# A chunked RWKV-7 recurrence with a SoLU layer behind it: whole products in the first doubling, transfers moved behind the read-out, a mean from a view, loads reordered

## The chip, the cores and the metric

The kernel runs on one core of one Trainium2 chip. The metric is the device time of one execution in microseconds (us); lower is better. A profile of one execution gives, for each engine, when each instruction ran and what it waited for. The engines are TensorE (PE for its matmuls, PEld for its weight loads), VectorE (DVE), ScalarE (ACT), GpSimd (POOL) and SyncE (SP), which issues nearly all DMA transfers here. A "q" behind a name (SPq, DVEq) is the engine's sequencer.

## The reference

A recurrence over 768 time steps, for 4 batches and 8 heads with a state of 40 x 40 each, is followed by a feed-forward layer on the 3072 rows of its output.

```python
for t in range(S):                       # r, k, v, w, a, b: (4, 8, 768, 40)
    y[:, :, t] = np.einsum('bhd,bhde->bhe', rt, state)
    Sa = np.einsum('bhde,bhe->bhd', state, at)
    state = state * wt[:, :, None, :] - np.einsum('bhd,bhe->bhde', Sa, bt) \
            + np.einsum('bhd,bhe->bhde', vt, kt)
x = y.transpose(0, 2, 1, 3).reshape(3072, 320)
h = x @ w_in                             # 320 -> 1024
sm = softmax(h)
solu = h * sm
ln = (solu - mean(solu)) / sqrt(var(solu) + 1e-6) * g_ln
out = ln @ w_out                         # 1024 -> 320
```

## The kernel before

**Chunks and rounds.** Time is cut into 12 rounds of 64 steps. A round's rows are loaded once, and it is worked in two chunks, each of two batches (the two halves of the 128 partitions) and all 8 heads. So there are 24 chunks, i = 0 to 23, and chunk i belongs to round i // 2. Inside a chunk the recurrence is written as matrix products. That needs, for each head and batch, the inverse of a 64 x 64 triangular matrix whose strict part is called nt.

**The stages of a chunk.** Each is a generator, and every `yield` ends a step:
- `front(i)`, five chunks ahead: logarithm of w (L334), cumulative sums on TensorE and their exponentials (pcum, pcx, L338 to L354), b and k scaled on POOL (L341), a copied on POOL (L371), a transposed (paT, evicted by DVE at L382), b transposed, nt (L292).
- `scatter` and `gather` write a round's nt to DRAM and bring its diagonal blocks back with one block in each partition.
- `invert(n)`: elimination on DVE in small steps (`prod`, `u`). Rounds 0 to 3 (`invert_fine`) do it for 16 x 16 blocks (14 pairs of steps), then ACT copies the result to u and ut (L441), and both go to DRAM (L443). Later rounds eliminate 32 x 32 blocks.
- `bring_inverse(i)` fetches the blocks as tinv and tinvT: eight transfers for a chunk.
- `solve(i)` doubles the inverse on TensorE: for the first rounds from 16 to 32 (py16, then pz16), for all from 32 to 64 (py, then pz). In the first doubling ACT evicts py16 to y_mid (L555); DVE adds the lower left part into tinv (L561, two instructions) and ACT writes the upper right part into tinvT (L565, four instructions). Both read the bank of pz16.
- `attend(i)`: transposes of k, v, r and the products that need no state (kT, vT, psi, rT, lamv, px0).
- `recurrence(i)` and `readout(i)`: the part that needs the state sm; its product nuT gives plamu, which comes once for each chunk and serves here as its mark in time. `readout` ends in x (L678), the chunk's y times the decays. x holds one round and has one buffer.
- `repack(n)` moves a round's x to xT, twelve transfers (L689 to L692), once both chunks of it are read out.
- `hidden(m)` and `output(m)`, six chunks behind (LAG = 6): h, softmax, product, statistics; then transposes (plnT) and the products with w_out (po). `centre()` folds g_ln and the mean over the features into w_out once, at chunk 6.
- `weights()` turns w_in and w_out from 64-bit numbers into 32-bit ones piece by piece (`narrow`), from a landing buffer of four pieces, with transfers three pieces ahead (L215).

**What sets the order.** The whole body is under a manual schedule: each engine, and each DMA queue, does its instructions in the order in which the program emits them. Strings of letters say how the steps of the stages interleave in a chunk: `EARLY` for chunks 0 to 5 and `STEADY` from 6. A letter is one step: r recurrence, y read-out, a `attend(i + 1)`, s `solve(i + 1)`, f and g fronts, I inverse (a number of steps given by `inverse_steps`), W weights, L loads, h hidden, b and o the end of the hidden layer and the output. An instruction that has to wait holds everything behind it on its engine. The small products of `solve` and the transposes share two PSUM banks (`bank`), so a bank that is not evicted holds TensorE.

Of the kernel before, what the change touches and what calls it, by code (L numbers as in the profile page):

```python
# [26 lines left out]
def shape_constants():  # L27

    s, t = np.arange(L)[:, None], np.arange(L)[None, :]
    first = (s < L // 2).astype(np.float64)
    two = np.eye(2)
    parts = dict(  # L40
        ident=np.eye(P),
        tri=np.concatenate([s < t, s < t], 0),
        cum_in=np.kron(two, first - (s <= t)),
        cum_ex=np.kron(two, (s < t) - first),
        half=np.concatenate([np.kron(two, 1 - first), np.kron(two, first)], 1),
        low=-1.0 * (np.arange(P)[:, None] % Q >= Q // 2),
    )
    at, where = 0, {}
    for name, x in parts.items():
        where[name] = (at, at + x.shape[1])  # L50
        at += x.shape[1]
    return np.concatenate([np.asarray(x, np.float64) for x in parts.values()], 1).astype(np.float32), where
# [3 lines left out]
def kernel(  # L56
# [37 lines left out]
    const = ctx.enter_context(tc.tile_pool(name="const", bufs=1))  # L94
    raw = ctx.enter_context(tc.tile_pool(name="raw", bufs=1))
    two = ctx.enter_context(tc.tile_pool(name="two", bufs=2))
    small = ctx.enter_context(tc.tile_pool(name="small", bufs=4))
    dram = ctx.enter_context(tc.tile_pool(name="dram", bufs=2, space=bass.MemoryType.DRAM))
    ps1 = ctx.enter_context(tc.tile_pool(name="ps1", bufs=2, space=PSUM))
    psd = ctx.enter_context(tc.tile_pool(name="psd", bufs=2, space=PSUM))  # L100
# [22 lines left out]
    def c_(name):  # L123
        lo, hi = where[name]
        return cst[:, lo:hi]
# [17 lines left out]
    x0_t = zeroed(nc.vector, "x0", [P, H, 64], 2, True)  # L143
    ti_t = zeroed(nc.vector, "tinvT", [P, 2, G, L], 2)
    tn_t = [const.tile([P, H, 2, Q // 2], FP32, name=f"tinv{i}") for i in range(2)]
    y_mid = const.tile([P, 2, G, Q], FP32, name="y_mid")
    w_in = const.tile([P, 5, DFF // 2], FP32, name="w_in")
    w2 = const.tile([P, NF, DM], FP32, name="w2")
    g_rows = const.tile([NF, P], FP32, name="g_rows")
    g_col = const.tile([P, NF], FP32, name="g_col")  # L150

# [86 lines left out]
    def centre():  # L238

        pg = bank("pg")  # L240
        nc.tensor.transpose(out=pg[:, 0:NF], in_=g_rows, identity=ident[0:NF, 0:NF])
        nc.scalar.copy(out=g_col, in_=pg[:, 0:NF])
        gb = two.tile([P, NF, P], FP32, tag="e", name="gb", bufs=1)
        nc.scalar.mul(out=gb, in_=g_col.unsqueeze(2).to_broadcast([P, NF, P]), mul=1.0 / DFF)
        yield
        t = bank("mean")
        for c in range(NF):
            nc.tensor.matmul(t[:, 0:DM], lhsT=gb[:, c, :], rhs=w2[:, c, :], start=c == 0, stop=c == NF - 1)
        mean = two.tile([P, DM], FP32, tag="osb", name="mean", bufs=1)
        nc.scalar.copy(out=mean, in_=t[:, 0:DM])  # L250
        yield
        for c in range(NF):
            nc.vector.scalar_tensor_tensor(out=w2[:, c, :], in0=w2[:, c, :], scalar=g_col[:, c:c + 1],
                                           in1=mean, op0=ALU.mult, op1=ALU.subtract)
            if c % 2:
                yield

    def half(p):
        return slice(64 * p, 64 * p + 64)
# [59 lines left out]
    def given(i, name):  # L319
        return of_round[i // 2][name][:, i % 2]  # L320
# [36 lines left out]
    def quarter(q):  # L357
        return slice(Q * q, Q * q + Q)
# [6 lines left out]
    def front(i):  # L365

        d = st[i]
        a = d["a"] = a_t[i % 2]
        parts = decay(i)
        next(parts)  # L370
        nc.gpsimd.tensor_copy(out=keyed(a)[:, :, :, 0:D], in_=by_heads(given(i, "a")))  # L371
        yield
        for _ in range(2):
            next(parts)
            yield
        next(parts)
        yield
        ax = d["ax"]
        t = bank("paT")
        for g in range(G):  # L380
            nc.tensor.transpose(out=t[:, g * P:(g + 1) * P], in_=pair(a, g), identity=ident)
        nc.vector.tensor_tensor(out=ax[:, :, 0:P], in0=t.rearrange("p (g t) -> p g t", g=G), in1=ax[:, :, P:2 * P],  # L382
                                op=ALU.mult)
        yield
        bT = transposed("bT", d["kb"][:, 1])
        yield
        n, s = divmod(i, 2)
        if s == 0:
# [27 lines left out]
    def invert_fine(n):  # L416
# [21 lines left out]
        for key, t, src in (("ut", ut, x.rearrange("b c t -> b t c")), ("u", u, x)):  # L438
            dst = of_round[n][key] = dram.tile([64, Q, Q], FP32, tag=key + "_dram", name=key + "_dram")
            for z in range(2):  # L440
                nc.scalar.copy(out=t[half(z)][:, :, R * z:R * z + R], in_=src[half(z)])  # L441
            for z in range(2):
                nc.sync.dma_start(out=dst[:, R * z:R * z + R, :], in_=t[half(z)])  # L443
        yield
# [80 lines left out]
    def solve(i):  # L525
# [20 lines left out]
        def whole(q):  # L546

            return (lambda p, g: nt[quarter(q), p, g, quarter(q % 2)],
                    lambda p, g: tinv[quarter(q), G * p + g].rearrange("s z c -> s (z c)"),
                    lambda p, g: tinvT[quarter(q), p, g, quarter(q % 2)],  # L550
                    lambda p, g: y_mid[quarter(q), p, g, :])

        if fine:
            t = products("py16", [(q, whole(q)[0], whole(q)[1]) for q in range(4)])
            nc.scalar.copy(out=y_mid, in_=t[:, 0])  # L555
            yield
            t = products("pz16", [(q, whole(q)[3], whole(q)[2]) for q in range(4)],
                         [(q, whole(q)[2], whole(q)[3]) for q in (0, 2)])
            for q in (0, 2):
                x = tinv[quarter(q), :, 0].rearrange("s (p g) c -> s p g c", p=2)  # L560
                nc.vector.scalar_tensor_tensor(out=x, in0=t[quarter(q), 1, :, :, 0:R], scalar=c_("low")[quarter(q)],  # L561
                                               in1=x, op0=ALU.mult, op1=ALU.add)
            for q in range(4):
                rows, c = slice(Q * q, Q * q + R), Q * (q % 2) + R
                nc.scalar.mul(out=tinvT[rows, :, :, c:c + R], in_=t[rows, 0, :, :, R:Q], mul=-1.0)  # L565
            yield

        def left(q):
# [201 lines left out]
    def fronts(i):  # L770

        return [j for j in ((4, 5) if i == 0 else (i + AHEAD,)) if j < N]

    EARLY = ("r r a W I r f W r r I W y r W a s f L a W I s W a f a W s I f a W s I f W f",
             "r r a W I r f W r r I g W y r I W a s f g L W a s a f g W a s f g W s a f g W f g W")
    STEADY = "r b r a r f b b o r o I o r o y o r I o h a f L a s a h f a I h f s h f h a f h"
    front_of = {}
    idle = ps2.tile([P, DFF], FP32, tag="h", name="idle")

# [19 lines left out]
    def warm(n, x):  # L799

        for _ in range(n):
            nc.tensor.matmul(idle[:, 0:512], lhsT=x[:, 0:P], rhs=x, start=True, stop=True)

    def later(n):
        load(n, "b", "k")
        yield

    with tc.manual_schedule():
# [14 lines left out]
        load(0, "r")  # L823
        gather(0)
        load(1, "k")
        turns("a f g a a f f W a g g", {}, f=f, g=g, a=at, W=ws)
        load(2, "w", "a")
        turns("I a I f g f g I f g", dict(I=[3, 4, 4]), f=f, g=g, I=inv, a=at)
        load(1, "v", "r")
        scatter(1)  # L830
        load(2, "b", "k")
        gather(1)
        turns("I a", dict(I=99), a=at, I=inv)
        warm(3, of_round[0]["spilt"])
        bring_inverse(0)
        begin(0)
        inv = inverses()
        turns("s W W W W s I s s I", dict(I=[4, 4]), s=so, I=inv, W=ws)
        after, before = None, None
        for i in range(N):  # L840
            m, more, js = i - LAG, i + 1 < N, fronts(i)
# [1 line left out]
            parts = dict(r=recurrence(i), y=readout(i), I=inv, W=ws, h=now, b=after, o=before)  # L843
            if i == LAG:
                steps(ws, 99)
                parts["o"] = centre()
            parts.update(zip("fg", (front_of[j] for j in js)))
            if more:
                parts.update(a=attend(i + 1), s=solve(i + 1))
# [4 lines left out]
            if i % 2 == 0:  # L854
                load((i + 6) // 2, "w", "a")
                parts["L"] = later((i + 6) // 2)
            turns(EARLY[len(js) - 1] if i < LAG else STEADY, dict(I=inverse_steps(i), s=2 if i == LAG else 1), **parts)
            if i % 2:
                if i + 2 < N:
                    bring_inverse(i + 2)  # L860
                load((i + 3) // 2, "v", "r")
                repack(i // 2)
            if js and js[-1] % 2:
                scatter(js[-1] // 2)
            begin(i + 1)
            after, before = now, output(m) if m >= 0 else None
        for m in range(N - LAG, N):
            now = hidden(m)
            turns("b h h o o h h b b h h o o o o", {}, h=now, b=after, o=before)
            after, before = now, output(m)  # L870
# [31 lines left out]
```

## Time and profile before

| | before |
|---|---|
| time, median of 3 runs | 742.56 us (741.05 to 743.6) |
| span of the profiled execution | 737.8 us |
| PE busy | 633.8 us (86%) |
| DVE busy | 432.0 us (59%) |
| ACT busy | 279.3 us (38%) |
| POOL busy | 102.0 us (14%) |
| mean granted TensorE clock | 0.905 |

The page's slices are 40 equal parts of the span (18.4 us each); a digit is a busy share in tenths, and PEclk is the clock that TensorE was granted, in tenths of full speed. In a row of the timeline stand the start, the duration, the engine, the line of the code, the operation and its tiles, and in brackets how long the engine sat idle before it and what ended the idle time. Rows of SPq are the issue of transfers, not the movement of their data. plamu of chunks 0 to 7 begins at 65.1, 91.8, 121.4, 156.1, 180.0, 214.7, 241.7 and 276.6 us.

### The profile page before, as it was taken

The page shows a single profiled execution, that of the slowest core. Times are in us where ns is not written, and L with a number is a line of the kernel's source. Part 1 is how long each engine was busy: PE and PEld are TensorE (multiplying, and loading weights), DVE is VectorE, ACT ScalarE, POOL GpSimd, SP SyncE. Part 2 cuts the span into 40 slices and gives each one's busy share as a digit, 9 for nine tenths or more (in the row PEclk, how much of TensorE's full clock was granted, in tenths as well). Part 3 has the DMA queues.
Part 4 walks back from the last instruction along what each step waited for, and adds up shares of the span by engine and source line. Part 5 has one row for each costly group of instructions (what it writes and reads, how often), then busy time and mean ns, then how long its engine had stood idle before and what let it go on. Part 6 is the DMA issues. An engine that isn't in the chain of part 4 may idle for free.

```text
span 737.8 us, 27981 instructions
## 1 busy us (share of the span) xinstructions
PE 633.8 (86%) x12165; PEld 451.7 (61%) x12165; DVE 432.0 (59%) x1186; ACT 279.3 (38%) x662; POOL 102.0 (14%) x192
## 2 busy tenths in 40 slices
PE   7547878388396879999999999999999899988997
PEld 4525657267375656776676767766676566554554
DVE  3417455355245756958869678598685872333442
ACT  4224634245342243435334443435243333322222
POOL 4211020120110102211122012202110000000000
PEclk9756887687676989999999999999999999999999
DMA  9874534643544425454553655545514322000001
GB/s 157 152 127 97 105 67 79 135 80 71 109 89 85 75 44 98 78 110 87 104 97 66 109 99 93 98 92 100 99 30 89 66 54 40 20 20 23 17 3 35
DMA packets 269866, 58.95 MB, mean 80 GB/s; under 512 B 255528, under 2 KB 265392, under 8 KB 269744
## 3 DMA queue, kind: packets, MB, share of 16 engines
q1 hardware_dynamic: 266480, 56.44, 41.0%
q8 instruction: 96, 1.57, 0.9%
q10 hardware_dynamic: 3264, 0.72, 0.6%
q14 instruction: 26, 0.21, 0.1%
HBM read 39.03 MB, written 13.37 MB: 71 GB/s over the span
## 4 chain that ended last, share of the span: by engine, by line
PE 61%; DVE 12%; ACT 6%; SPq 6%; issue 4%; DMA 3%; DVEq 0%; ACTq 0%
PE po L744 13%; PE h L699 12%; PE pyo L671 4%; PE plnT L739 3%; PE pcx L351 3%; DVE prod L465 3%; PE pz L539 2%; DVE u L467 2%; PE py L539 2%; PE plamv L290 2%; DVE nmax L709 2%; PE pcum L338 2%; DMA blk<-blk_dram 2%; PE ppsi L290 2%; PE pyo L593 2%
## 5 line engine op out<-in xcount | busy, mean ns | idle before, releaser
L699 PE MATMUL h<-w_in,xT 128*128 128x512 f32 (+1 forms) x288 | 128.6, 636 | 3.9 <-DVE e L716 3.9
L744 PE MATMUL po<-w,lnT 128*128 128x320 f32 x384 | 115.6, 440 | 0.0
L744 PEld LDWEIGHTS po<-w,lnT 128*128 128x128 f32 x384 | 69.5, 192 | 26.4 <-issue 3.3
L467 DVE TENSOR_TENSOR u<-u,prod 128x30 f32<-128x30 f32 (+7 forms) x240 | 65.1, 271 | 8.2
L465 DVE TENSOR_TENSOR prod<-blk,u 128x30 f32<-128x30 f32 (+7 forms) x240 | 65.5, 273 | 7.1
L351 PE MATMUL pcx<-cst,lw 128*128 128x132 f32 x192 | 35.0, 316 | 37.5 <-ACT tinvT L565 31.1
L341 POOL TENSOR_TENSOR kx<-raw_b,inv 128x320 f32<-128x320 f32 x24 | 20.7, 867 | 289.7 <-ACT inv L339 227.4
L351 PEld LDWEIGHTS pcx<-cst,lw 128*128 128x128 f32 x192 | 29.5, 214 | 47.1 <-ACT tinvT L565 35.0
L709 DVE TENSOR_REDUCE nmax<-h 128x1 f32<-128x1024 f32 x24 | 29.3, 1221 | 47.9 <-PE h L699 47.9
L699 PEld LDWEIGHTS h<-w_in,xT 128*128 128x128 f32 (+1 forms) x288 | 38.0, 190 | 31.4 <-issue 29.4
L678 DVE TENSOR_TENSOR x<-pyo,kx 128x512 f32<-128x512 f32 x24 | 16.6, 691 | 69.3 <-PE pyo L671 46.8
L749 ACT ACTIVATE osb<-po,rs 128x320 f32<-128x320 f32 x24 | 12.6, 527 | 97.2 <-PE po L744 86.4
L740 ACT COPY lnT<-plnT 128x512 f32<-128x512 f32 x48 | 27.5, 586 | 33.6 <-PE plnT L739 33.5
L713 ACT ACTIVATE e<-h,nmax 128x1024 f32<-128x1024 f32 x24 | 26.7, 1114 | 34.4 <-DVE nmax L709 34.4
L292 DVE TENSOR_TENSOR lamv<-plamv,cst 128x512 f32<-128x512 f32 x24 | 16.6, 691 | 39.2 <-PE plamv L290 39.2
L716 DVE TENSOR_TENSOR e<-h,e 128x1024 f32<-128x1024 f32 x24 | 29.4, 1225 | 14.6 <-ACT e L713 14.0
L539 PE MATMUL py<-tinv,nt 32*32 32x32 f32 x1280 | 28.4, 204 | 9.1 <-DMA tinv<-ut_dram 7.4
L731 POOL TENSOR_TENSOR rs<-c,mhalf 128x1 f32<-128x1 f32 x24 | 13.2, 548 | 157.2 <-DVE c L730 157.2
L739 PE MATMUL plnT<-cst,e 128*128 128x128 f32 x192 | 29.5, 282 | 5.7 <-DVE e L716 5.4
L581 ACT ACTIVATE tinvT<-pz 32x256 f32<-32x256 f32 x48 | 17.9, 373 | 43.5 <-PE pz L539 43.2
L657 POOL TENSOR_TENSOR sm<-tot,fac 128x320 f32<-128x320 f32 x20 | 14.9, 745 | 126.3 <-DVE tot L656 109.0
L539 PEld LDWEIGHTS py<-tinv,nt 32*32 32x32 f32 x1280 | 23.6, 115 | 14.3 <-DMA tinv<-ut_dram 9.0
(121 smaller groups left out, 1181.1 us busy)
## 6 DMA issues: line engine op xcount, KB each, us to landing
blk<-blk_dram SPq DMA_DIRECT2D x16, 256.0 KB
raw_k<-in_k_dram SPq DMA_DIRECT2D x24, 160.0 KB
v<-in_v_dram SPq DMA_DIRECT2D x24, 160.0 KB
r<-in_r_dram SPq DMA_DIRECT2D x24, 160.0 KB
out_dram<-osb SPq DMA_DIRECT2D x24, 160.0 KB
raw_w<-in_w_dram SPq DMA_DIRECT2D x23, 160.0 KB
raw_b<-in_b_dram SPq DMA_DIRECT2D x23, 160.0 KB
raw_a<-in_a_dram SPq DMA_DIRECT2D x23, 160.0 KB
```

What stands on the lines that cost most here:

```text
L290: nc.tensor.matmul(t[half(c ^ p * cross), p, g * L:(g + 1) * L], lhsT=lhs[half(p), g, half(c)], rhs=rhs[half(p), g, half(c)], start=True, ...
L351: nc.tensor.matmul(t[:, g * 132:g * 132 + 132], lhsT=pair(lw, 2 * j + g), rhs=cst[:, lo:lo + 132], start=True, stop=True)
L465: nc.vector.tensor_tensor(out=t, in0=nb[:, j:j + 1, j + 1:Q].to_broadcast([P, rows, m]), in1=u[:, 0:rows, j:j + 1].to_broadcast([P, rows, ...
L467: nc.vector.tensor_tensor(out=u[:, 0:rows, j + 1:Q], in0=u[:, 0:rows, j + 1:Q], in1=t, op=ALU.subtract)
L539: nc.tensor.matmul(t[quarter(out), c:c + Q], lhsT=lhs(p, g), rhs=rhs(p, g), start=True, stop=True)
L671: nc.tensor.matmul(t[half(p), c, g * W:g * W + used], lhsT=kb[half(c), j, 2 * g + p, :], rhs=lam[half(c), h % 2, h // 2, 0:used], start=i ...
L699: nc.tensor.matmul(h[:, j * 512:j * 512 + 512], lhsT=of_round[i // 2]["xT"][rows, kt, i % 2 * P:i % 2 * P + P], rhs=w_in[rows, 4 if kt == ...
L709: nc.vector.tensor_reduce(out=nmax, in_=h, axis=AX.X, op=ALU.max, negate=True)
L716: nc.vector.tensor_tensor(out=q, in0=h, in1=e, op=ALU.mult)
L739: nc.tensor.transpose(out=t[:, j * P:(j + 1) * P], in_=q[:, f * P:(f + 1) * P], identity=ident)
L740: nc.scalar.copy(out=lnT[:, fs.start:fs.stop].rearrange("p f t -> p (f t)"), in_=t)
L744: nc.tensor.matmul(o[:, 0:DM], lhsT=lnT[:, f, :], rhs=w2[:, f, :], start=f == 0, stop=f == NF - 1)
```

## The change

It has five parts.
- **The first doubling.** A constant tile y_16 has the right half of a unit matrix in its right columns. One DVE instruction evicts py16 into its left columns, with the unit matrix added and the sign set (`low` is -1 for the lower rows and 0 for the upper). The products of pz16 with y_16 are then whole: both results are plain copies, on ACT, and DVE no longer adds into tinv.
- **Transfers of y.** `repack` gets a letter of its own, X, directly behind the read-out of an odd chunk, in place of its call at the chunk's end behind the transfers of the next inverse and the loads.
- **The mean of w_out.** The matmuls of `centre` take g_col as weights through a view that repeats one column 128 times, in place of a tile gb that ACT filled; the factor 1/1024 moves to the mean's eviction. The first step of `centre` comes at the end of chunk 5.
- **The start.** The first inverse is emitted in one piece, before the steps of the fronts that surrounded it; its transfers come before scatter and loads of round 1; the loads of round 2's w and a come earlier, others later; five warm-up matmuls replace three.
- **Orders.** In `EARLY` a step of `attend` (r transposed) stands ahead of pz16; in chunk 6 the four steps of `solve` are spread. The copy of a moves one step later in `front`. The pool `small` has 3 buffers in place of 4.

```diff
+        one=np.kron(np.ones((4, 1)), np.eye(Q)),
...
-    small = ctx.enter_context(tc.tile_pool(name="small", bufs=4))
+    small = ctx.enter_context(tc.tile_pool(name="small", bufs=3))
...
+    y_16 = const.tile([P, H, Q], FP32, name="y_16")
+    nc.scalar.copy(out=y_16[:, :, Q // 2:], in_=c_("one")[:, Q // 2:].unsqueeze(1).to_broadcast([P, H, Q // 2]))
...
-        gb = two.tile([P, NF, P], FP32, tag="e", name="gb", bufs=1)
-        nc.scalar.mul(out=gb, in_=g_col.unsqueeze(2).to_broadcast([P, NF, P]), mul=1.0 / DFF)
...
-            nc.tensor.matmul(t[:, 0:DM], lhsT=gb[:, c, :], rhs=w2[:, c, :], start=c == 0, stop=c == NF - 1)
+            nc.tensor.matmul(t[:, 0:DM], lhsT=g_col[:, c:c + 1].to_broadcast([P, P]), rhs=w2[:, c, :], start=c == 0, stop=c == NF - 1)
...
-        nc.scalar.copy(out=mean, in_=t[:, 0:DM])
+        nc.scalar.mul(out=mean, in_=t[:, 0:DM], mul=1.0 / DFF)
...
         next(parts)
+        yield
+        next(parts)
         nc.gpsimd.tensor_copy(out=keyed(a)[:, :, :, 0:D], in_=by_heads(given(i, "a")))
         yield
-        for _ in range(2):
-            next(parts)
-            yield
+        next(parts)
+        yield
...
-                nc.scalar.copy(out=t[half(z)][:, :, R * z:R * z + R], in_=src[half(z)])
+                if n == 0 and key == "ut":
+                    nc.vector.tensor_copy(out=t[half(z)][:, :, R * z:R * z + R], in_=src[half(z)])
+                else:
+                    nc.scalar.copy(out=t[half(z)][:, :, R * z:R * z + R], in_=src[half(z)])
...
-                    lambda p, g: y_mid[quarter(q), p, g, :])
+                    lambda p, g: y_16[quarter(q), G * p + g, :])
...
-            nc.scalar.copy(out=y_mid, in_=t[:, 0])
+            nc.vector.scalar_tensor_tensor(
+                out=y_16[:, :, 0:R], in0=t[:, 0].rearrange("q p g c -> q (p g) c")[:, :, 0:R], scalar=c_("low"),
+                in1=c_("one")[:, 0:R].unsqueeze(1).to_broadcast([P, H, R]), op0=ALU.mult, op1=ALU.add)
...
-            for q in (0, 2):
-                x = tinv[quarter(q), :, 0].rearrange("s (p g) c -> s p g c", p=2)
-                nc.vector.scalar_tensor_tensor(out=x, in0=t[quarter(q), 1, :, :, 0:R], scalar=c_("low")[quarter(q)],
-                                               in1=x, op0=ALU.mult, op1=ALU.add)
             for q in range(4):
                 rows, c = slice(Q * q, Q * q + R), Q * (q % 2) + R
-                nc.scalar.mul(out=tinvT[rows, :, :, c:c + R], in_=t[rows, 0, :, :, R:Q], mul=-1.0)
+                nc.scalar.copy(out=tinvT[rows, :, :, c:c + R], in_=t[rows, 0, :, :, R:Q])
+            for q in (0, 2):
+                nc.scalar.copy(out=tinv[quarter(q), :, 0].rearrange("s (p g) c -> s p g c", p=2),
+                               in_=t[quarter(q), 1, :, :, 0:R])
...
-    EARLY = ("r r a W I r f W r r I W y r W a s f L a W I s W a f a W s I f a W s I f W f",
-             "r r a W I r f W r r I g W y r I W a s f g L W a s a f g W a s f g W s a f g W f g W")
-    STEADY = "r b r a r f b b o r o I o r o y o r I o h a f L a s a h f a I h f s h f h a f h"
+    EARLY = ("r r a W I r f W r r I W y r X W a s f L a W I a s W f a f W s I a f W s I f W",
+             "r r a W I r f W r r I g W y r I W a s f g L W a a s f g W a f g W s a f g W s f g W")
+    STEADY = "r b r a r f b b o r o I o r o y o r X I o h a f L a s a h f a I h f s h f h a f h"
...
-        turns("a f g a a f f W a g g", {}, f=f, g=g, a=at, W=ws)
         load(2, "w", "a")
-        turns("I a I f g f g I f g", dict(I=[3, 4, 4]), f=f, g=g, I=inv, a=at)
-        load(1, "v", "r")
+        turns("a f g a a f f a g g W", {}, f=f, g=g, a=at, W=ws)
+        turns("I a f g f g f g a", dict(I=99), f=f, g=g, I=inv, a=at)
+        warm(5, of_round[0]["spilt"])
+        bring_inverse(0)
         scatter(1)
-        load(2, "b", "k")
+        load(2, "b")
+        load(1, "v")
         gather(1)
-        turns("I a", dict(I=99), a=at, I=inv)
-        warm(3, of_round[0]["spilt"])
-        bring_inverse(0)
+        load(1, "r")
+        load(2, "k")
         begin(0)
         inv = inverses()
-        turns("s W W W W s I s s I", dict(I=[4, 4]), s=so, I=inv, W=ws)
+        turns("W W s W W s W W I s I s", dict(I=[4, 4]), s=so, I=inv, W=ws)
...
-                parts["o"] = centre()
+                parts["o"] = middle
...
+            else:
+                parts["X"] = repacked(i // 2)
+            order = EARLY[len(js) - 1] if i < LAG else STEADY
+            if i == LAG:
+                order = order.replace("a s a h f a I h f s h f h", "a s a h f s a I h f s h f s h")
+            turns(order, dict(I=inverse_steps(i)), **parts)
             if i % 2:
                 if i + 2 < N:
                     bring_inverse(i + 2)
                 load((i + 3) // 2, "v", "r")
-                repack(i // 2)
...
+            if i == LAG - 1:
+                middle = centre()
+                steps(middle, 1)
```

More of the change, by code (lines that the diff above doesn't have):

```diff
@@ L802, in warm, with repacked @@
             nc.tensor.matmul(idle[:, 0:512], lhsT=x[:, 0:P], rhs=x, start=True, stop=True)
+    def repacked(n):
+        repack(n)
+        yield
     def later(n):
@@ L856 @@
                 parts["L"] = later((i + 6) // 2)
-            turns(EARLY[len(js) - 1] if i < LAG else STEADY, dict(I=inverse_steps(i), s=2 if i == LAG else 1), **parts)
+            else:
[4 more added lines that the diff above has]
+            turns(order, dict(I=inverse_steps(i)), **parts)
             if i % 2:
```

## The prediction

> **What bounds the kernel now.** I read the page's slices first, then the busy time by stretches of one chunk each (cut where plamu, one per chunk, starts), then the waits, the timeline around the longest one, and the DMA queue's own timeline.
>
> ```profile
> PE   7547878388396879999999999999999899988997
> PEclk9756887687676989999999999999999999999999
> ```
> ```profile
> 65.00:92.00 27.00, 20.09 (x574) 16.61 (x576) 15.18 (x41) 15.35 (x41) 4.60 (x7) 0.86 0.54 106
> 92.00:121.00 29.00, 21.96 (x550) 18.29 (x546) 17.59 (x57) 11.48 (x32) 4.09 (x9) 0.71 0.33 64
> 121.00:156.00 35.00, 21.29 (x596) 17.57 (x598) 12.14 (x40) 14.02 (x39) 3.66 (x6) 0.71 0.56 111
> 156.00:180.00 24.00, 19.42 (x597) 16.16 (x593) 14.95 (x55) 11.29 (x33) 4.63 (x10) 0.79 0.35 65
> 180.00:215.00 35.00, 22.14 (x617) 18.32 (x613) 12.14 (x40) 14.13 (x38) 3.66 (x6) 0.66 0.55 107
> 277.00:658.00 381.00, 368.75 (x7250) 259.95 (x7242) 265.82 (x708) 151.06 (x349) 54.22 (x96) 1.00 0.42 79
> ```
> Columns after the length: PE, PEld, DVE, ACT, POOL, clock, DMA share, GB/s. From 277 us on TensorE is 97% busy at clock 1.00 (23.8 us a chunk): nothing in the change takes work from it there, so I expect nothing from those 461 us. Before 277 us no engine is full, the clock is 0.66 to 0.86, and chunks 2 and 4 take 35 us against 24 for chunk 3, which has the same work.
>
> ```profile
> PE pcx L351 <- ACT tinvT L565: 31.1, 6, 10.2
> ```
> ```profile
> 130.74 0.69 PE L539 MATMUL pz<-y_mid,tinvT 32*32 32x32 f32 x31 [1.51 <-issue]
> 131.36 0.66 PE L271 MATMUL prT<-cst,r 128*128 128x128 f32 x4
> 142.22 1.25 PE L351 MATMUL pcx<-cst,lw 128*128 128x132 f32 x4 [10.21 <-ACT tinvT L565]
> ```
> ```profile
> 133.98 1.38 SPq L316 DMA_DIRECT2D raw_w<-in_w_dram  x2
> 135.24 0.69 DVE L678 TENSOR_TENSOR x<-pyo,kx 128x512 f32<-128x512 f32 x1 [10.89 <-DMA xT<-x]
> 138.75 0.69 DVE L561 SCALAR_TENSOR_TENSOR tinv<-pz,cst,tinv 32x128 f32<-32x128 f32 x2
> 138.88 1.27 ACT L441 COPY ut<-u 64x256 f32<-64x256 f32 x2 [10.48 <-DVE u L435]
> 141.02 1.14 ACT L565 ACTIVATE tinvT<-pz 16x128 f32<-16x128 f32 x4
> ```
> The last releaser is not the cause. TensorE waits for a bank read by L565; ACT is held in order at L441 by the inverse on DVE; DVE stands at L678, because x has one buffer and the xT transfers of the chunk before still read it. They were issued at 123.42 to 133.88, behind everything else of the DMA queue. The same at chunk 4 (10.96 us).
>
> The start is a queue too:
> ```profile
> 38.25 2.44 SPq L399 DMA_DIRECT2D blk_dram<-nt  x4
> 44.13 1.62 SPq L409 DMA_DIRECT2D blk<-blk_dram  x2
> 45.85 1.42 SPq L443 DMA_DIRECT2D ut_dram<-ut  x2
> 49.32 1.79 SPq L486 DMA_DIRECT2D tinv<-ut_dram  x4
> ```
> The first inverse is ready at 39.0, its copies at 41.1, but its write leaves at 45.85, since scatter, loads and gather of round 1 stand before it.
>
> [...] (clock 0.50 from 135 to 140) [...] 0.50 still at 145 to 150 with PE busy 4.74 of 5. [...] here ut's issue ends at 47.27 and its reader starts at 49.32. [...] the trace has L565 begin (58.57) only after L561 ends (58.49).
>
> **Part by part.**
> *Transfers of y behind the read-out.* The 12 transfers (10.5 us of issue at chunk 1) move to directly behind x, before the second half of the chunk. x of the next chunk then finds its buffer free. At chunk 2, DVE could start x at 125.0; the following rows (x 0.69, tot 0.48, weights 1.4, psi 0.68, weights 0.5, inverse 0.35: starts overlap, 3.5 us from 135.24 to 138.75) end near 129, ACT's four copies 2.1 us later, then rT's 0.58: pcx near 132 instead of 142.2. Gain 9.7. The stretch 142 to 154 at half clock (PE busy 11 us) would at full clock take some 7: 4 more, an estimate. Chunks 2 and 4: 2 x 13.5 = 27. What is queued behind them on the DMA queue: weight fetches (three pieces ahead, as many as the rest of the chunk uses) and the next inverse's transfers, needed a chunk later.
>
> *First doubling as whole products.* One DVE instruction per chunk replaces ACT's y_mid copy (0.372); the two DVE L561 (0.34 each) become two ACT copies. Not seen in the trace: the eviction of 128x128 from PSUM. [...] upper 0.48, row L656 with 320 elements. I take 0.34. It stands behind x and before psi and the inverse, and pz16 comes two steps later, so it is hidden. L565 then no longer waits for a DVE that is in the inverse, and rT goes ahead of it. The waits this ends: 1.5 at 81.7 (chunk 0), 2.9 at 106.6 with half clock to 120 (chunk 1: 5 in all), 2.5 at 166.6 (chunk 3: 3), 2.5 at chunk 5, 4.3 and 1.2 at chunk 6. ACT's extra 0.6 before the left half's products is charged in the allowance below.
>
> *Mean from a view.* ACT gb (1.06) and its wait (0.7) go, 1.7 in chunk 6; the 16 matmuls (4.6) stay, with weights read from one column; [...] I take as now. With the solve of chunk 6 spread, chunk 6 gains 8.
>
> *Start.* The whole inverse runs at once on DVE: in round 1's rows the same 28 steps take 6.5 us, so done near 33, ut copied by DVE by 33.6, its write 12.2 us earlier. Behind it wait paT's evictions (two times 0.69) and the fronts of 2 and 3, hence TensorE idles to 34 and has 5 us of work (now 32.65 to 37.6), then five warm-up matmuls (ten passes, 0.81 each by 4.84 for six): free near 46.7. py16, its eviction, then pz16 at 48 instead of 55.9. From there to plamu 9.2 us at half clock, near 8 warm. First plamu at 56 instead of 65.1: gain 9. The fill of y_16 waits on ACT for the constants; at most 0.5 us ahead of the first Ln at 6.33.
>
> *The rest.* raw_a is freed one step later, on POOL behind grown b; the load that waits for it has a chunk of slack. small with 3 buffers: each value lives one chunk. Both cost nothing.
>
> *Sum.* 9 + 1.5 + 5 + 13.5 + 3 + 13.5 + 2.5 + 8 = 56. From it I take an allowance of 8. The DMA queue issues about 42 us for a pair of early chunks (sum of its rows from 152 to 204, without waits), while these gains would leave pairs of 42 to 46 us: it becomes nearly the bound, and some waits like that at 97.7 and 98.5 (tinv, 2.0 us at chunk 1) must appear. So 48: 742.6 - 48 = 695.
>
> **Rivals.**
> *The queue takes the place of x's wait.* The moved transfers push back fetches and tinv; each even chunk then loses some 3 us at tinv, as chunk 1 does now (idle at 96.1 and 98.1, landed at 98.5), and stays at half clock. Left: 2 x 6.5 at x, 9 at the start, 4 at chunk 6: 26, so 717. For it: 42 us of issue. Against: counted from the nt that ends an even chunk, the queue does scatter (2.8), eight inverse transfers (4), gather (2.2), xT (10.5) and fetches (2 to 4), so the next eight leave at 22 to 28, while py16 of the following chunk comes at about 29 (one chunk of 21, and 8 from nt at 152.3 to py16 at 160.3).
> *The clock stays up.* The 8 are not given back and half-clock stretches (115 to 120, 170 to 178, 227 to 240) go as well: 60 or more, 682. Against: gaps of 1.5 us put down to "issue" stay.
> *Slower.* Eviction on DVE, longer warm-up and weight fetches behind 10 us of transfers stall DVE in order, and the gain of the start is lost: about 748. Against: in-order DVE has 12 to 15 us of work in 35.
>
> **How the numbers follow.** Forecast 0.62, queue 0.20, clock 0.13, slower or nothing 0.05. The range 676 to 723 holds the first three cases, with 6 us around the outer two. Faster 0.94, same 0.02, slower 0.04.
>
> **What would show it.** DVE x waiting for xT: from 21.9 us to under 3. PE waiting for L565: from 31.1 to under 8. First plamu at 54 to 58, that of chunk 7 near 229 (276.6 now). Clock over 0.8 in 120 to 230. From there to the end 461 us as now. Wrong, if plamu of chunks 2 and 3 is still over 30 us apart, or if DMA tinv or fetches head the waits.

## The result, and the profile after

| | before | after |
|---|---|---|
| time, median of 4 runs | 742.5 us (741.05 to 743.6) | 714.0 us (711.51 to 716.53) |
| ratio to before, 95% interval | | 0.962 (0.957 to 0.966) |
| span of the profiled execution | 737.8 us | 709.6 us |
| PE busy | 633.8 us | 634.4 us |
| mean granted clock | 0.905 | 0.923 |

The change is faster by 28.5 us. TensorE is busy as long as before; what went is its idle time, 104.0 us of the span before and 75.2 after. The forecast was 695, a gain of 48.

The page's slices of after (17.7 us each), engine and clock:
```profile
PE   7566877898875999999999999999999899979997
...
PEclk9676699687899599999999999999999999999999
```
Busy time by stretches from one plamu to the next (chunks 0 to 6, then the rest to chunk 23). After the length stand PE, PEld, DVE, ACT, POOL, clock, DMA share and GB/s:
```profile
58.70:91.20 32.50, 25.10 (x569) 20.66 (x568) 18.29 (x50) 15.31 (x41) 5.39 (x8) 0.70 0.59 116
91.20:114.40 23.20, 17.71 (x565) 14.57 (x569) 15.81 (x52) 11.82 (x35) 4.33 (x9) 0.93 0.40 84
114.40:140.60 26.20, 21.63 (x602) 18.12 (x598) 13.71 (x44) 14.10 (x39) 3.88 (x6) 0.74 0.78 141
140.60:161.40 20.80, 18.95 (x594) 15.85 (x586) 14.53 (x53) 11.31 (x33) 4.69 (x10) 0.84 0.41 87
161.40:185.20 23.80, 21.45 (x602) 17.99 (x592) 12.93 (x42) 13.99 (x39) 3.76 (x6) 0.71 0.77 132
185.20:214.10 28.90, 22.39 (x612) 17.38 (x606) 12.37 (x39) 9.75 (x27) 4.63 (x8) 0.94 0.48 87
214.10:249.10 35.00, 27.06 (x613) 19.22 (x607) 22.50 (x56) 10.40 (x28) 2.21 (x5) 0.76 0.31 57
249.10:622.20 373.10, 361.05 (x7138) 254.38 (x7134) 266.19 (x703) 150.05 (x346) 54.45 (x96) 1.00 0.46 81
```
Before, these chunks took 26.8, 29.6, 34.7, 23.9, 34.7, 27.0 and 35.0 us. Chunks 1 to 4 together fell from 122.9 to 94.0. Start and chunk 0 together are what they were (91.8 and 91.2): plamu of chunk 0 comes 6.4 us earlier, and chunk 0 is 5.7 longer. Chunks 5 and 6 together rose from 62.0 to 63.9. So the whole gain lies in four chunks. Of its 28.9 us there 23.9 are idle time of TensorE (38.2 us before, 14.3 after); the other 5.0 are shorter busy time, at a mean clock of 0.80 in place of 0.71.

TensorE's longest waits up to 285 us, after (us in total, times, longest):
```profile
PE pz L545 <- issue: 12.7, 5, 7.0
PE pbT L273 <- DVE kx L385: 5.4, 1, 5.4
PE pu L639 <- DVE x L620: 4.6, 2, 3.2
PE pyo L678 <- DVE lamu L294: 3.3, 1, 3.3
PE py L545 <- DMA tinv<-ut_dram: 3.1, 2, 2.0
```
The 31.1 us of pcx behind L565 are gone, and so are the 21.9 us of DVE's x behind xT. The list shows what stands in their place. Chunk 2, at the rows that answer to those of before (x at 135.24 after a wait of 10.89, pcx at 142.22 after 10.21):
```profile
119.19 0.69 DVE L685 TENSOR_TENSOR x<-pyo,kx 128x512 f32<-128x512 f32 x1 [0.51 <-PE pyo L678]
...
124.46 1.27 ACT L447 COPY ut<-u 64x256 f32<-64x256 f32 x2 [1.54 <-DVE u L438]
...
125.94 0.24 PE L545 MATMUL pz<-tinvT,y 32*32 32x32 f32 x3 [1.67 <-issue]
...
126.61 0.59 ACT L275 COPY rT<-prT 128x512 f32<-128x512 f32 x1
...
127.25 1.25 PE L353 MATMUL pcx<-cst,lw 128*128 128x132 f32 x4 [0.16 <-ACT rT L275]
```
pcx begins 12.8 us after chunk 2's plamu, where it was 20.8. Its bank is now free as soon as rT is copied, ahead of the solve's copies. But rT itself stands on ACT behind the four copies of ut and u, so that the gap of 1.67 ahead of pz16 did not set when pcx began: without it pcx would have waited longer for rT. And the four pcx matmuls take 1.25 us, as long as before: the clock was 0.50 in both (from 142.0 to 143.5 before, from 127.0 to 128.5 after).

### The profile page after: what moved, and what is told of

It reads as the page before. It is cut to its first block, busy times and chain, and to the rows that moved or that the text cites. A ratio compares the mean times of both kernels' runs of the same rounds, so it can differ in the third digit from the quotient of the medians.

```text
span 709.6 us, 27985 instructions
## 1 busy us (share of the span) xinstructions
PE 634.4 (89%) x12169; PEld 451.3 (64%) x12169; DVE 434.2 (61%) x1180; ACT 279.1 (39%) x668; POOL 103.3 (15%) x192
## 3 DMA queue, kind: packets, MB, share of 16 engines
q8 instruction: 96, 1.57, 1.0%
## 4 chain that ended last, share of the span: by engine, by line
PE 67%; DVE 13%; ACT 5%; SPq 5%; DMA 5%; issue 5%; POOL 0%; ACTq 0%; DVEq 0%; POOLq 0%
PE po L751 15%; PE h L706 14%; PE pyo L678 5%; PE plnT L746 4%; PE pcx L353 3%; PE py L545 2%; DVE prod L471 2%; PE plamv L292 2%; PE pz L545 2%; DVE u L473 2%; DVE nmax L716 2%; SPq L318 2%; PE ppsi L292 2%; PE pyo L600 2%; PE pcum L340 2%
## 5 line engine op out<-in xcount | busy, mean ns | idle before, releaser
L706 PE MATMUL h<-w_in,xT 128*128 128x512 f32 (+1 forms) x288 | 130.4, 643 | 3.9 <-DVE e L723 3.9
L343 POOL TENSOR_TENSOR kx<-raw_b,inv 128x320 f32<-128x320 f32 x24 | 21.1, 878 | 305.0 <-ACT inv L341 270.9
L685 DVE TENSOR_TENSOR x<-pyo,kx 128x512 f32<-128x512 f32 x24 | 16.6, 691 | 46.7 <-PE pyo L678 45.8
L720 ACT ACTIVATE e<-h,nmax 128x1024 f32<-128x1024 f32 x24 | 26.8, 1116 | 34.0 <-DVE nmax L716 34.0
L545 PE MATMUL py<-tinv,nt 32*32 32x32 f32 x1280 | 26.5, 200 | 5.9 <-DMA tinv<-ut_dram 3.1
L728 DVE BATCH_NORM_STATS2 bs<-e 128x6 f32<-128x512 f32 x48 | 30.9, 685 | 0.8
L746 PEld LDWEIGHTS plnT<-cst,e 128*128 128x128 f32 x192 | 22.1, 143 | 13.9 <-ACT sT L631 4.0
```

What stands on the lines that cost most here:

```text
L545: nc.tensor.matmul(t[quarter(out), c:c + Q], lhsT=lhs(p, g), rhs=rhs(p, g), start=True, stop=True)
L706: nc.tensor.matmul(h[:, j * 512:j * 512 + 512], lhsT=of_round[i // 2]["xT"][rows, kt, i % 2 * P:i % 2 * P + P], rhs=w_in[rows, 4 if kt == ...
L728: nc.vector.bn_stats(out=bs[:, j], in_=q[:, j * 512:j * 512 + 512])
L746: nc.tensor.transpose(out=t[:, j * P:(j + 1) * P], in_=q[:, f * P:(f + 1) * P], identity=ident)
```

## The experiments

The experiments ran in three groups of four (e1 to e4, e5 to e10, e11 to e14), each on one chip with the kernel before beside it; each ratio is to that. The changed kernel was measured by itself in the same way. The three sums are from the profiled execution of each: to chunk 1's plamu, chunks 1 to 4, chunks 5 and 6. The last column has TensorE's idle time in chunks 1 to 4 and the mean clock there.

| kernel | median us | ratio (95%) | start and 0 | 1 to 4 | 5 and 6 | 1 to 4: TensorE idle, clock |
|---|---|---|---|---|---|---|
| changed | 714.0 | 0.962 (0.957 to 0.966) | 91.2 | 94.0 | 63.9 | 14.3, 0.80 |
| e1 transfers alone | 727.7 | 0.979 (0.976 to 0.982) | 94.5 | 108.3 | 62.2 | 21.1, 0.70 |
| e2 all but the transfers | 726.7 | 0.977 (0.973 to 0.981) | 90.9 | 112.3 | 58.2 | 37.2, 0.79 |
| e3 old start | 715.0 | 0.961 (0.955 to 0.968) | 93.0 | 98.4 | 63.4 | 19.7, 0.83 |
| e4 chunk 6's solve early | 704.8 | 0.948 (0.944 to 0.953) | 90.7 | 92.1 | 56.4 | 19.4, 0.89 |
| e5 old doubling | 708.3 | 0.955 (0.951 to 0.959) | 92.6 | 93.0 | 60.2 | 16.3, 0.83 |
| e6 gather earlier | 705.9 | 0.952 (0.948 to 0.955) | 87.1 | 95.1 | 59.3 | 18.2, 0.84 |
| e9 e4 and fillers | 704.9 | 0.952 (0.948 to 0.957) | 92.1 | 94.2 | 54.5 | 11.5, 0.93 |
| e10 e4 and inverse in the mean | 703.1 | 0.948 (0.945 to 0.952) | 89.9 | 98.2 | 53.5 | 17.4, 0.79 |
| e11 transfers and orders alone | 710.6 | 0.958 (0.953 to 0.964) | 93.7 | 97.0 | 59.4 | 15.3, 0.77 |
| e12 old orders | 716.2 | 0.964 (0.960 to 0.969) | 90.1 | 98.6 | 64.0 | 21.4, 0.83 |
| e13 e6 and e10 | 697.4 | 0.937 (0.933 to 0.942) | 88.3 | 96.8 | 50.6 | 17.3, 0.81 |
| e14 e13, old doubling | 701.0 | 0.945 (0.941 to 0.949) | 88.3 | 99.1 | 47.8 | 21.8, 0.85 |

How far one profile's sums can be trusted shows in e4 and e10: their code is the same up to the end of chunk 4, and chunks 1 to 4 took 92.1 in the one and 98.2 in the other. The idle time does not account for it (19.4 and 17.4); the granted clock was 0.89 in the one and 0.79 in the other. Differences of under some 6 us in such a sum settle nothing; the medians do.

**e1: the transfers alone, on the kernel before.**
```diff
-    EARLY = ("r r a W I r f W r r I W y r W a s f L a ...
+    EARLY = ("r r a W I r f W r r I W y r X W a s f L a ...
...
+                parts["X"] = repacked(i // 2)
...
-                repack(i // 2)
```


> The kernel before with only the twelve xT transfers moved directly behind the read-out; all else as before. Theory A (the gain is mostly the read-out's wait for its buffer, 10.9 us at each of chunks 2 and 4): 722 to 728 us, the intervals of chunks 2 and 4 fall from 34.7 to 25 to 27, the start stays at 65. Theory B (the transfers' place alone only moves the wait into the DMA queue, so that the whole products and the new start have to carry the gain): 735 us or more, with chunks 2 and 4 still over 31.

727.7: the transfers alone bring about 15.6 us, in chunks 2 (34.7 to 27.7) and 4 (34.7 to 25.4). x at chunk 2 begins after 0.73 us of idle time. Theory A holds, with chunk 2 just above its range. The clock in chunks 1 to 4 is as low as before (0.70 and 0.71), and TensorE's longest waits there are behind ACT, in e1's waits from 92 to 215 us:
```profile
PE pcx L351 <- ACT tinvT L565: 8.2, 4, 3.3
PE pz L539 <- issue: 3.9, 2, 2.1
PE pnt L290 <- ACT bT L273: 2.7, 4, 0.7
```

**e2: the changed kernel with the transfers back at the chunk's end.**
```diff
-            else:
-                parts["X"] = repacked(i // 2)
...
+                repack(i // 2)
```


> The changed kernel with the xT transfers put back at the end of the odd chunks, behind everything else of the queue. Theory A: 732 to 737 us (18 to 23 more than the changed kernel), the read-out waits again some 10 us in chunks 2 and 4. Theory B: under 722 us, since the whole products and the start keep their gain and nothing stands on ACT any more.

726.7, some 13 us more than the changed kernel; A expected 18 to 23 and B expected it under 722, so the size fits neither. The mechanism is A's: DVE waits again. DVE's and TensorE's waits of e2, up to 285 us and from 92 to 190:
```profile
DVE x L685 <- DMA xT<-x: 25.5, 2, 12.9
```
```profile
PE pz L545 <- DVE y L561: 23.3, 2, 11.7
PE pcx L353 <- ACT rT L275: 4.6, 2, 2.3
```
The pair shows what the whole products do to a wait on DVE. In the kernel before TensorE met it by way of ACT, at pcx; now that DVE itself evicts py16, TensorE meets it directly and earlier, at pz16. Here the products remove no wait for DVE; they move it.

**e3: the start of the kernel before in the changed kernel.**
```diff
-        turns("I a f g f g f g a", dict(I=99), f=f, g=g, I=inv, a=at)
-        warm(5, of_round[0]["spilt"])
-        bring_inverse(0)
-        scatter(1)
+        turns("I a I f g f g I f g", dict(I=[3, 4, 4]), f=f, g=g, I=inv, a=at)
+        load(1, "v", "r")
+        scatter(1)
...
```


> The changed kernel with the start of the kernel before: order of the first loads, of the first inverse and of the warm-up, and ut's copy on ACT. Theory A (the 6.4 us that the start gains are given back in chunk 0, where gather, bits and the inverse of round 1 come no earlier): within 2 us of the changed kernel (712 to 716), first plamu near 65 and the second near 92. Theory B (the start's gain is real and chunk 0 loses for another reason, the whole products' eviction on DVE): 719 to 723 us, second plamu near 97.

715.0, and plamu at 67.2 and 93.0. A holds: the 6.4 us by which the new start brings the first plamu forward (8.5 against e3) are worth about 1 us, not to be told from nothing. Chunk 0 of the changed kernel shows where they go:
```profile
49.55 1.45 SPq L412 DMA_DIRECT2D blk<-blk_dram  x2
...
55.36 3.46 SPq L219 DMA_DIRECT2D bits<-in_moe_w_in_dram  x6
```
```profile
54.72 0.29 DVE L426 TENSOR_SCALAR u<-blk 128x256 f32<-128x256 f32 x1 [4.14 <-DMA blk<-blk_dram]
...
59.64 0.76 DVE L170 TENSOR_SCALAR parts<-bits 128x256 int32<-128x256 int32 x1 [1.33 <-DMA bits<-in_moe_w_in_dram]
...
64.06 0.68 DVE L294 TENSOR_TENSOR lamu<-plamu,cst 128x512 f32<-128x512 f32 x1
```
```profile
64.89 1.67 PE L678 MATMUL pyo<-lamu,kx 64*64 64x104 f32 x32 [3.27 <-DVE lamu L294]
```
plamu ran at 58.7, but its eviction lamu stands on DVE behind an inverse and weights that wait for transfers of the same queue. Those come later than before: blk, the blocks of round 1, is issued at 49.55, where it was issued at 44.13, because the transfers of the first inverse now stand ahead of it.

**e6: gather of round 1 one load earlier, loads of r and k behind the first fetches of w_in.**
```diff
         load(2, "b")
-        load(1, "v")
         gather(1)
-        load(1, "r")
-        load(2, "k")
+        load(1, "v")
...
         turns("W W s W W s W W I s I s", dict(I=[4, 4]), s=so, I=inv, W=ws)
+        load(1, "r")
+        load(2, "k")
```


> The changed kernel with two changes of the first loads: the gather of round 1 directly behind the load of b (one load earlier), and the loads of r (round 1) and k (round 2) behind the first fetches of w_in. Theory A (chunk 0 gives the start's gain back because DVE waits 4.1 us for round 1's blocks and 1.3 for w_in, with lamu behind them on DVE): chunk 0 falls from 31 to 33 to some 28, 709 to 712 us. Theory B (chunk 0 is set by something else, the half clock or the DMA queue as a whole, so that the wait only moves): 713 us or more.

705.9, better than A expected. e6's rows show blk's wait at 0.58 in place of 4.14. The wait for w_in remains (1.62 at 56.58), but it is over before plamu:
```profile
51.37 0.29 DVE L426 TENSOR_SCALAR u<-blk 128x256 f32<-128x256 f32 x1 [0.58 <-DMA blk<-blk_dram]
...
60.57 0.69 DVE L294 TENSOR_TENSOR lamu<-plamu,cst 128x512 f32<-128x512 f32 x1 [1.00 <-PE plamu L292]
```
lamu waits for its own product, and chunk 0 falls from 32.5 to 27.7. So the start's gain can be had, once the transfers that DVE needs in chunk 0 come first. The rest of the gain (chunks 5 and 6) is not explained by this edit.

**e4: the first step of chunk 6's solve ahead of the second group of inverse steps.**
```diff
-  order.replace("a s a h f a I h f s h f h", "a s a h f s a I h f s h f s h")
+  order.replace("r X I o h a f L a s a h f a I h f s h f h", "r X s I o h a f L a a h f s a I h f s h f s h")
```


> The changed kernel with the first step of chunk 6's solve (the whole products py16 and their eviction y_16 on DVE) put ahead of the second group of inverse steps instead of behind it. Theory A (chunk 6 kept its 35 us because y_16's eviction stands on DVE behind seven inverse steps, TensorE idles 7 us and then runs at half clock to 245): 704 to 708 us, chunk 6's interval 25 to 29. Theory B (chunk 6 is held by the mean, the scatters and the inverse themselves): 712 us or more, chunk 6 still over 33.

704.8, and chunk 6 takes 26.1 us in place of 35.0. The rows of the changed kernel that A rests on, TensorE's and then DVE's:
```profile
222.47 0.70 PE L353 MATMUL pcx<-cst,lw 128*128 128x132 f32 x4
230.16 1.07 PE L545 MATMUL pz<-tinvT,y 32*32 32x32 f32 x64 [6.99 <-issue]
```
```profile
223.83 0.27 DVE L471 TENSOR_TENSOR prod<-blk,u 128x110 f32<-128x110 f32 x1
...
229.11 0.68 DVE L294 TENSOR_TENSOR psi<-ppsi,cst 128x512 f32<-128x512 f32 x1
229.71 0.34 DVE L561 SCALAR_TENSOR_TENSOR y<-py,cst 128x128 f32<-128x128 f32 x1
```
"issue" only says that the profile has no releaser. pz16 reads y_16, and y_16 ends at 230.05. From 223.83 to 229.1 DVE did seven inverse steps, emitted ahead of it. In e4 y_16 stands before them:
```profile
222.36 0.48 DVE L663 TENSOR_TENSOR tot<-pyo,sm 128x320 f32<-128x320 f32 x1
222.76 0.34 DVE L561 SCALAR_TENSOR_TENSOR y<-py,cst 128x128 f32<-128x128 f32 x1
223.02 0.26 DVE L471 TENSOR_TENSOR prod<-blk,u 128x110 f32<-128x110 f32 x1
```

**e5: the first doubling of the kernel before, all else as changed.** py16 is copied to y_mid by ACT, DVE adds into tinv, ACT writes tinvT with -1.

> The changed kernel with the first doubling of the kernel before (py16 copied to y_mid by ACT, the product subtracted from tinv on DVE, tinvT written by ACT with -1 behind it); all else as changed. Theory A (the whole products gain what they gain in chunks 1 and 3, where ACT and then TensorE waited for the DVE of the inverse, and lose in chunk 6, where y_16 now stands on that DVE): 718 to 722 us, chunk 1 at 28 or more (23.3 in the changed kernel), chunk 3 at 24 to 27, chunk 6 at 32 to 35. Theory B (the order of chunks 1 and 3 and the early xT are what shortens them): 712 to 715 us, chunk 1 under 25.

708.3: both theories fall, and chunk 1 at 26.5 fits neither. The two intervals (0.951 to 0.959, and 0.957 to 0.966 for the changed kernel) overlap by little, so the old doubling is probably the faster one here and not the slower. Chunks 1 to 4 are as short (93.0 and 94.0), and chunk 6 takes 28.5 in place of 35.0: with y_mid copied by ACT, pz16 has no wait of 7 us there. If the products do not shorten chunks 1 to 4, what does? The new step orders had not been tried yet.

**e11: transfers and the new `EARLY` strings on the kernel before; e12: the old `EARLY` strings (with X) in the changed kernel.**
```diff
-  "... X W a s f L a W I s W a f a W s I f a W s I f W f"
+  "... X W a s f L a W I a s W f a f W s I a f W s I f W"
```


> The kernel before with the early transfers and the changed kernel's order of the steps in chunks 0 to 5 (rT ahead of the solve's second step), and nothing else: first doubling, start and mean as before. The early transfers alone gave 727.7 us, the changed kernel 714.0, and the changed kernel with the old doubling 708.3, so the products are not what makes the difference. Theory A2 (the order does, because rT and the pcx behind it no longer wait for ACT to copy the first doubling): 714 to 719 us, chunks 1 to 4 together 96 to 101 (108.3 with the transfers alone, 94.0 in the changed kernel). Theory B2 (the new start and the order of the first loads do, in chunks 1 to 4 as well): 724 us or more, chunks 1 to 4 still over 105.

> The changed kernel with the order of the steps in chunks 0 to 5 as before (the early transfers stay). Theory A2 (the order carries what the transfers do not): 721 to 727 us, chunks 1 to 4 over 104. Theory B2 (start and loads carry it, or the whole products do so only without the new order): 712 to 717 us.

e11 gives 710.6 with nothing but the two re-orderings: better than A2 expected, and at least as fast as the whole change. So the products, the mean and the start, as they stand in the changed kernel, add nothing to the median that can be seen. e12 gives 716.2 with the old order: only 2 us more than the changed kernel, not to be told from nothing, and the number of B2. So the order is enough, as e11 shows, but with the rest of the change in place it is not needed.

The two do not work in the same way. Against e1, which has the transfers alone, e11 cut the idle time of TensorE in chunks 1 to 4 from 21.1 to 15.3 us: rT, and pcx behind it, get past ACT's copies of the first doubling. e12 left it at 21.4. Its stretch is 9.7 us shorter than e1's at a clock of 0.83 in place of 0.70. Why the clock was higher stays open: e12 has the new start and the products together, no run has the transfers with the products alone, and e4 and e10 show that the clock can differ by 0.10 in the same code. TensorE's waits for ACT from 92 to 215 us, in e11 and in e12:
```profile
PE pcx L351 <- ACT rT L273: 2.0, 2, 1.8
PE paT L381 <- ACT tinvT L565: 2.0, 1, 2.0
```
```profile
PE pcx L353 <- ACT tinv L571: 6.3, 4, 2.2
PE pnt L292 <- ACT bT L275: 3.7, 5, 0.7
```
The old order shows the wait at pcx again, four times as in e1, now behind the plain copies of tinv, and little shorter than the 8.2 us of e1.

**e9: on e4, fillers in TensorE's waits of chunks 1 to 5** (results read by nobody).
```diff
+            for _ in range(2):
+                nc.tensor.matmul(idle[:, 0:480], lhsT=cst[:, 0:P], rhs=cst[:, 0:480], start=True, stop=True)
...
+  order.replace("r r a W I r f W r r I W y", "r r a M W I r f W r M r I W y")
```


> The version with chunk 6's solve early (704.8 us), and in chunks 1 to 5 twice two matmuls of 480 columns whose result nobody reads, in TensorE's waits ahead of pu and of pyo. It tells what the half clock in chunks 1 to 5 costs. Theory A (the stretches at half clock behind those waits, 5 to 13 us each in chunks 2, 4 and 5, cost the 4 us apiece that the forecast counted): 695 to 701 us, clock near 1.00 from 110 to 200. Theory B (the clock falls at the later gaps within the runs of 32x32 products, or the fillers take the place of useful work): 704 to 712 us.

704.9, as e4: B. In chunks 1 to 4 of its profile TensorE idled less than in e4 (11.5 and 19.4 us) at a higher clock (0.93 and 0.89), yet the stretch was no shorter (94.2 and 92.1). That the fillers keep the clock up was not shown. In chunk 2 it was 1.00 where they stand (114.1 to 116.0), but in the changed kernel, which has none, it was 1.00 from 109 to 125 as well; and with them it was 0.52 from 127 on. e9's chunk 2, by stretches:
```profile
113.50:120.00 6.50, 5.93 (x200) 4.43 (x192) 4.95 (x17) 2.41 (x7) 1.35 (x2) 1.00 0.59 89
120.00:127.00 7.00, 4.53 (x181) 3.73 (x173) 3.71 (x12) 4.20 (x12) 2.35 (x4) 1.00 1.08 138
127.00:134.00 7.00, 6.75 (x173) 5.74 (x168) 2.68 (x8) 4.76 (x14) 0.00 (x0) 0.52 0.89 180
```
Within 120 to 127 TensorE had two gaps, 0.90 (issue) and 1.52 (ACT rT, behind ACT's copies of ut and u).

**e10: on e4, the inverse steps in the stretch of the mean.**
```diff
-            return [0, 0, 4, 5, 5]
+            return [0, 0, 4, 5, 0]
+        if i == LAG:
+            return [12, 3, 4, 4]
...
-  "r b r a r f b b o r o I ..."
+  "r b r a r I f b b o r o I ..."
```


> The version with chunk 6's solve early (704.8 us), with the last five inverse steps of chunk 5 and most of chunk 6's moved to the stretch in which TensorE computes the mean and DVE has nothing (0.4 to 1.3 us busy of 5). Theory A (x0 and y_16 stand on DVE behind inverse steps: 3.5 us of TensorE's wait ahead of pu, then the mean at part of the clock, and 2.0 us at prT): chunks 5 and 6 fall from 56.3 together to 50 to 53, 699 to 702 us. Theory B (the mean's matmuls and the transfers set the length of these two chunks): 704 us or more.

703.1, between the two expectations: chunks 5 and 6 fell from 56.4 to 53.5 in the profiles, and the wait of pu for x0 is gone, but the medians of e4 and e10 do not differ by more than their spread.

**e13 and e14: what helped, together.**

> The changed kernel with all that helped: gather of round 1 one load earlier with r and k behind the weights' first fetches, chunk 6's solve early, and the inverse steps of chunks 5 and 6 moved into the mean. If the three gains stand on different waits (chunk 0, chunk 5, chunk 6): 694 to 699 us. If they only shift where the clock falls to a half: 701 us or more.

> The same with the first doubling of the kernel before in place of the whole products. With y_16's eviction no longer held by the inverse in either, theory A (the products cost only by chunk 6) expects it 2 us or more slower than the one with whole products; if the whole products cost time in the other chunks too, as the run with the old doubling hints (708.3 against 714.0), it is equal or faster: 690 to 698 us.

e13 gives 697.4 (0.933 to 0.942), the fastest here and 5.8 to 6.7% less than before: the gains of chunk 0 and of chunks 5 and 6 stand on different waits and add up. The same with the old doubling gives 701.0. Their intervals overlap by little (0.941 to 0.942), so the whole products may be worth a few us once chunk 6 is put right, as A had it for this pair. The two profiles do not show where: chunks 5 and 6 are the shorter ones in e14.

## Why the prediction was right or wrong

The direction, the cause at chunks 2 and 4 and the rest of the program (461 us from chunk 7 on, measured 460.5) were right. The size was not: 28.5 of 48. By stretches the sum of 56 had 10.5 for the start and chunk 0, 35 for chunks 1 to 4 and 10.5 for chunks 5 and 6. The profiles have 0.6, 28.9 and a loss of 1.9. So the allowance of 8 covered what was missing in chunks 1 to 4, and the rest is missing at the two ends. By terms:

*Transfers behind the read-out, 27 before the allowance.* Mechanism right, shown by e1 and e2: 15.6 alone, about 13 when taken out of the whole. pcx at chunk 2 came 8.0 us earlier in its chunk, where 9.7 was forecast for it; on the path to it pyo waits 1.57 us, since lamu stands behind weights on DVE (0.52 before), and a gap put down to issue takes 1.18 (0.76 before). The 4 us for the clock in each of chunks 2 and 4 did not come: from 127 to 140 TensorE was busy 12.84 of 13 us at 0.51, and from 170 to 185 14.40 of 15 at 0.54. This term was mis-sized: chunks 2 and 4 gave 8.5 and 10.9, not 13.5 each. That the allowance of 8, meant for a fuller queue, covered it is luck. The queue itself cost little: TensorE's waits for DMA tinv went from 7.4 to 3.1 us.

*Whole products.* "It stands behind x and before psi and the inverse" is the step that failed. In chunks 1 to 4 it holds: no wait of TensorE there names y_16, whose eviction takes 0.35 us (forecast 0.34, at most 0.48). In chunk 6 `STEADY` emits two groups of inverse steps ahead of it, and TensorE idles 7.0 us and then runs at a clock of 0.50 to 245. The 8 us forecast for chunk 6 became none; e4 took 8.9 off it. At chunk 5 the wait for L565 before was 1.39 (at 227.0), not the 2.5 of the sum. And the credit for chunk 1 went to the wrong part: e11 has it without the products (23.6). Chunk 3 is less plain. It took 19.5 to 22.5 us in all nine profiles with the whole products and 23.9 to 26.9 in the five without. But chunk 2 goes the other way (21.1 in e5, 20.6 in e14, 26.2 in the changed kernel), and the two chunks together took 46.7, 46.3 and 47.0 us, so no gain of the products is left there.

*Mean from a view.* It was not tried alone. Its 16 matmuls took 6.16 us against 4.58; the shortest took 432 ns in both, and the clock was 0.53 from 207.7 to 211.1, after pu's wait of 3.17 for x0 behind inverse steps on DVE. In e10, without that wait, the 16 took 4.47. So the view itself is as cheap as taken, and the 1.7 came with that wait. The mean also moved from chunk 6's stretch to the end of chunk 5's (207.7 to 213.9), so chunk 6 kept its 35.0 without it, and only the sum of the two chunks can be compared.

*Start, 9.* plamu at 58.7, forecast 56. The sum then took chunk 0 as 25.3 from there, without asking what else chunk 0 needs. It was 32.5. The term failed on round 1's transfers, which the new order puts behind those of the first inverse and which DVE needs before lamu; e3 shows that the start is then worth about 1 us, and in e6, with blk earlier, chunk 0 takes 27.7.

*Signs named beforehand.* First plamu: 58.7, just outside 54 to 58. Chunk 2's and chunk 3's: 26.1 apart, under the 30 that would have been wrong. x waiting for xT: gone. pcx waiting for L565: gone, but pz16 has 7.0 in its place. plamu of chunk 7 at 249.1, not 229. Clock from 120 to 230: 0.82. No fetch heads the waits.

Of the rivals, "the queue takes the place" came nearest in number (717) but not in cause.

## What to carry to other kernels

When an eviction moves to another engine, read its place in that engine's order in every schedule string of the program, not in one: on an in-order engine its price is what stands ahead of it (7.0 us here), not its own 0.35. Moving a start forward is worth only as much as the transfers that the next stage needs move with it. And before a new algorithm gets the credit for a wait removed, try the re-ordering that came with it alone: here it did as much as the whole. Compare medians before the stretches of one profile: here the same code differed by 6 us in a stretch of 92, at clocks of 0.89 and 0.79 (e4 and e10).

## What was not expected of the hardware

*The clock's return.* In the changed kernel the clock stayed at 0.50 for long after the 7 us wait of chunk 6, and for a short time in the mean:
```profile
230.00:245.00 15.00, 14.45 (x261) 9.54 (x265) 4.67 (x13) 3.90 (x12) 0.00 (x0) 0.50 0.16 37
208.20:211.30 3.10, 3.10 (x8) 1.90 (x7) 0.00 (x0) 0.22 (x1) 1.25 (x2) 0.50 0.95 145
```
From 230 to 245 TensorE was busy 14.45 of 15 us at 0.50. In the mean it was busy 3.10 of 3.10 us at 0.50 from 208.2 to 211.3, and the clock was 1.00 again from 211.8 to 214.0. What decides between the two no run here shows. Nor did the clock fall only behind a wait as long as that of 7 us: in chunk 2 it was 1.00 up to 126.0 and 0.50 from 126.2 to 127.0, and TensorE's longest gap between 109 and 126.2 was 1.67 us.

*Gaps at fixed counts of instructions.* TensorE's gaps of up to 2.7 us (2.73 in e4, at 51.46) put down to issue fall on the same instruction in kernels of the same TensorE program, at other times: before three pz products in chunk 2 (1.67 in the changed kernel, 1.72 in e4), before the last 19 plamv in chunk 3 (1.24 and 1.45), before 24 of pz's products in chunk 4 (1.47 and 1.18). It is the count that is fixed, not the place in the program, as e9 shows without having been made for it. Its fillers put 16 matmuls and 16 weight loads ahead of chunk 2's pz16, and the gap stands 16 products earlier:
```profile
123.49 0.35 PE L545 MATMUL pz<-tinvT,y 32*32 32x32 f32 x19 [0.90 <-issue]
```
Busy time and instructions up to this gap and up to one in chunk 5 (PE, PEld and so on as above), in the changed kernel and then in e9:
```profile
0.00:125.90 125.90, 90.56 (x1999) 69.20 (x2000) 68.50 (x211) 52.22 (x134) 29.15 (x60) 0.81 0.71 122
0.00:195.10 195.10, 153.01 (x3779) 121.57 (x3780) 103.76 (x326) 89.56 (x236) 40.98 (x82) 0.79 0.68 121
```
```profile
0.00:123.45 123.45, 91.44 (x1999) 68.13 (x2000) 66.94 (x210) 51.27 (x132) 28.80 (x60) 0.85 0.72 122
0.00:196.50 196.50, 155.02 (x3779) 116.64 (x3780) 104.04 (x330) 89.35 (x236) 40.59 (x82) 0.87 0.68 121
```
The other two gaps of the changed kernel come after 2635 and 3144 matmuls. From gap to gap that is 636, 509 and 635 matmuls and as many weight loads, 1272, 1018 and 1270 instructions: within two of 5, 4 and 5 times 254. The profile's page lists a queue for instructions (packets, MB, share of 16 engines):
```profile
q8 instruction: 96, 1.57, 1.0%
```
That is 16 KB a packet. If the queue is TensorE's, which the profile does not say, its 24338 instructions by 96 packets are 254 for each, an estimate from the page's counts (12169 matmuls and as many weight loads). That these are waits for the next piece of the program is the author's guess from the two numbers; no run shows it. The data queue was not full ahead of the gap in chunk 3: from 149.0 to 151.2 the DMA engines were busy 0.13 of the time.
